# A kernel's order table of 1,771 steps replaced by another, with new durations in its planner

## The chip, the cores and the metric

The kernel runs on one core of a Trainium2 chip. The metric is the device time of one execution in microseconds (us). Besides its times there is one execution that the hardware profiler recorded; its page and its trace are quoted below.

## The reference

Two parts follow each other. The first is a linear attention with a decaying state (r, k, v, w: 4 batches, 8 heads, 768 tokens, 48 channels; u: one row for each head):

```python
for t in range(S):
    cur = np.einsum('bhd,bhe->bhde', u[None] * kt, vt)
    y[:, :, t] = np.einsum('bhd,bhde->bhe', rt, state + cur)
    state = wt[:, :, :, None] * state + np.einsum('bhd,bhe->bhde', kt, vt)
...
x = attn_out.transpose(0, 2, 1, 3).reshape(B * S, H * D)   # 3072 x 384
h = x @ w_in                                               # 384 x 2048
g = h * np.clip(h + 3.0, 0.0, 6.0) / 6.0
return g @ w_out                                           # 2048 x 384
```

Everything is float32; the weights arrive as 64-bit floats and are turned into float32 on the chip.

## The kernel before

**Work.** The tokens are cut into 24 chunks of 128 (`i`), four of which make a block (`bk`, six of them). For a chunk the kernel scans the decays backwards and forwards (`back`, L431; `fore`, L440), multiplies them onto k and r (`K`, L451; `R`, L455), works out the token's own term (`own`, `dot`, `sum`, `diag`: L464, L476, L482, L492), the scores inside the chunk (`score`, L501; masked into place by `above`, L508), turns K round (`turn`, L517; copied by `turned`, L522), multiplies it with v (`kv`, L601; copied by `kvs`, L612) and carries the state (`decay`, `mid`, `decb`, `state`: L530, L538, L546). The chunk is read out by L579 and L588. For chunks 0 and 1 this is `first`, after `clear` (L652) has started the accumulation and before `read` (L660) has put the last heads in place through a copy by ACT (`third`, L646).

**The two big products.** Block 0 computes them plainly (`up0`, L717, one step for each of 16 column groups and part of the tokens; `ramp` and `gate`, L707 and L728, are the activation; `down0`, L736). The five other blocks use fewer products on sums of the operands: 20 products for each half d of the columns (`up1.0.*`, `up1.1.*`, L832), whose results ACT and DVE add together (`read`, L847 and L849) before the activation (`clip`, `gate`, L853 and L857), and 7 products for the second weight (`down`, L887) on sums made by DVE (`sum`, L872). The sums of the weights themselves are made once by DVE (`sin`, L779 to L783; `sout`, L808). Each weight comes in 8 pieces: `fetch` (SP, L394) loads one into one of three `bits` buffers, ACT makes two halves of it (`low`, `sign`: L403, L408), DVE a third (`shift`, L414) and joins them (`full`, L418). Late in the program weights and decays are loaded again and looked at for values that the fast path cannot take (`vet`, L935).

**What sets the order.** Each piece of work is a step of a `Plan`: an engine, a planned duration, the steps that it needs, the buffers it holds. `Plan.order` does not search: it reads for each step its place from the table `ORDER` (two characters a step) and lays all steps in that sequence. Every engine then runs its own steps in it, one after another; a step that waits holds up all that stand behind it on its engine. SP's queue of loads is one of these engines. The planned durations, `RATE` (a load of kb kilobytes takes kb/RATE in the plan) and `LAND` give planned starts. With a given table these have one use only: before a PE step that is planned to start in the first 60 us, `Plan.emit` puts products of the identity with itself, whose result nobody reads (`spin`, L1269), one after another as long as the planned gap lasts. So the durations decide how many spins are in the program, and the table decides everything else.

There are four PSUM buffers called `bank`; an `up` holds one until its `gate` has read it, a `score` two until `above` has.

```python
rank = [CODE.index(ORDER[2 * i]) * 64 + CODE.index(ORDER[2 * i + 1]) for i in range(len(steps))]
...
out = [n for _, n in sorted(zip(rank, steps))]
...
while now < self.start[n] - 0.12:
    self.spin()
    now += next(us_ for upto, us_ in self.SPIN if now < upto)
```

Of the kernel before, what the change touches and what calls it, by code (L numbers as in the profile page):

```python
# [86 lines left out]
    "HVHiHWHyH2H9IrJWJlJtJ0GHHdGIG/HmItIyHGGtHNIPIVJcIDINIHIYIcKMLfLkG3IKG9HzILI/JCH3HZHjJeJjLnIvJbIwJgJiLxMAMLMWMQHnJdHo"
    "JvJ4K/LDJ1IBIdLqLuMIKTLtLwL1MRMfMmI4LlI6KHLmL6MBKOJUJnMFMPMpL4MJMbMiMwOrO5PAPHLHMGLKLrMHMZMeLyLZL0MtMxO1MYMrL9MvMzM5"
    "PFP5QELSMnLVMNMoM/NGMUL2MTOyPEP9M3O4M2PkPlPoQQQXQcQrQkNWO0NYOOOzPTPXOUN2OBP8QAQdPLQDPMQHQKQRQyRARHN+P/OAPdP+QWQaPhOc"
    "PNQlQpRLQVQoQYQqQtQuRtScSpSuS2ODQeOGQCQfQ8RCQMPQQGRQRTSkQ2RNQ4RXRZRdTZURUZRERIRMRgRmR9SCRlR0SDSiSxUWRwSnRxT/UBUDUjUx"  # L90
    "VCVIVMR3SjR5S0TKTyT2S8SSSdUeUhU3TgUVTeUbUdUiVKVUVdSIUYSLTUUXUwU0TYSmS6U2U+VfUpU7UuU/VDVJVyYEYGYUYKSVU4SbUfU5VPVSUlS/"
    "UmVkVpYHVOVbVRVmVqYOYRYYT6VcT7VAVeV3V9VHUoVEYMYQYcV2YLV6YNYSYfYiYkYrYnBCABAEArAuAsA2AGA4A7AwBAAHBDBHA6BPBBB1B+B7CFCD"
    "ClCoCmCwA0CTCZBrChBLCHCKCQC6CVC0C5DNDSD8EhEmEfEsDPDzD2D1EcCgD/EBDQEkCsDfDiDpDtEpE/FCE+FgEGErEvEwE2E1FKFOFLFVDvE3E6En"
    "FABGBMBWB3B8B/EUEbEiBZBhBtBkBxB0FaFhFiBbBiBoBnCCCPEAEIELBEBKBYBsByB2EHEPERB6CECIEeEoEuBwB5B9ExFIFRCMCeCjENESEWCfCtCz"
    "EQEVEYC3C/DEFSFYFbC8DIDOElEtEyCkCxDFD0D7ECCqDbDhEaEgEjDJDTDaG+HKHQDUDeDmE4E9FDDlDxD3EqEzE7DdDnDrD5EFEME8FBFHFjFtF0F6"
    "F/GCGEGBGFGKGMGRGbGeGmGuGvGsGwGyG4HBHJHUHaHrH6HgHlHqHwH1H5ICIGITIXD4D6FEFGFJFNFTFqGOGQGTGUHDHEHFHIHLHSHTHfHpHtHuHvHx"
    "H4H7H8H+IAIRIUIWIaIgIhIjIkIlInJNJPFsF1GAGGGJGLKDKhIFIOIpI5IeIuI2JGJqI+JAJLIQISI7IMIiImIZIzJDJOJRJkIqI0IxIbI8IsI9JEIo"
    "IfJYJQI3JBJIJVJXJpJ5KBKFJZKAJTJrJFJKJwJzJ6J9JMJSI1JHJ7KIKdKkKrJaJfKuJ+KEKXJmJxKGJuJ2KCKUKSKaJ/KRKKJsKiKJKYKqJ3JyKoKz"
    "J8KcKLKjKVKmKxK0K4KZKeK5K9KfKlKsKvKpKtKwK1KPKbKNLOLMLULCLGLLLYKnLAK2LELILNLQLTLWLaLbLjL3L5LFLJLXLRLcLpL8LdL+LeLhLvMC"
    "LgLiL/MMKgKyLoLsK7K8L7MDMKMOMXMaMlM8K3LzMSLBMVMgNBMdNDMkMsMyM9NPNTNcNmNvNpNrN1MqNANeMuM4NHM1NJNQNjNXNiNRNZNVM0NfNLNb"  # L100
    "NwNCM6NqN6NONlNUNuNdNyN3OQOqNhNkOKOTNoNsNtN0N4OLNzOFNaNgN9OHOSOhOpOXOaOjNxN5OPN7OCOMNENNOeOxOmO2OEONOIN/OZOROVOfOJNI"
    "OkOnOYOdOiO3OwO8PBPIPOPCPGOtO6OgOlOoOsO/PDOvO9OWObOuPjPJPqPVPZPgPtO7PRO+PYPePiPmPpPrPvPxP0P7QBPcPfPsPnP1P6QLP3QNPyP4"
    "QOQZPzP2QTQmPKPPQFQJPUPWQUQbQiQsQnQvQ1Q7PSQSQjPbQwQzQ+Q0Q/Q5RGRPRURSRcRkRvR7RFRKR4RoRrR1Q9RORYRVRhR/SRSUShRaRiRuRBRp"
    "RfRjRqRWRbR2R8RnR6SKSWSZSoSrStSySeSgSFSJSTSvSQSaS3S9RsSBRzSNSwS7TDTTTdSzS4TlSqSsTMR+SMSESGSYSlTFS+TJS1TBTASATISHTPTf"
    "SXSOTXTqSfTRS5TLTETNToTrTvTGTbTtTwTVTaTcTiTQTSTjTmTCTHTkTsT8UHT1T5UAUKTWT0TxT3T9UCUEUGUIULUMUUUgUqT4T+UJUFUNUcUtUPUv"
    "UOUSUkUrUQUTUzVGTOThUaUsTpTuUnU1U8VQVBVFVNVaTnUyU9TzVVVLViVYVlVXVhVoVtV1V8WZWiWsXNXQXbVgVjWEVnVxV4VrWBWPWVWWWdV5WCV/"
    "VsWeV+WFXVVzVwWmXhWIWOWTWgWYWhW0W4W8WaWcXlXnWQWSWpWuWkWoXYXcWDWGWlWvXEXLXTXmXpXzWMWRW2VuWHWJWXWfWnWyW9XHWrW1WwWAXIWN"
    "W6XrWKWbXOX3WjW7WtXKXBXMXXXaXfXDXFX4X6W+XCXRXUXPXSXsXuWzW3YPYXYeYmYVYZYhYqXqX7YWYdYAYFYjYlYoYuYsYtYxY8X+YgYpYJYyYvY/"
    "Y1ZBWqWxW/XoXZXgXkX1XAXWW5XeXvXwXiXxXtYIX2X5X9X/XdXjX0XyYTX8YBYaYbYCYDYwYzY3Y6ZDZHZLZOZoY2Y5ZcaPaWaeY0Y9ZMY7ZAZJZYZU"
    "ZfZGZKaZY4ZNZPZRZWZCY+ZTZgZEakZQZdZZZjZuZwZzZeZiZkZpanavZXZbZqZtZaZmabadZFZSZ+aKaYZ0Z7aCaTaaalZlZxZvZhZsZ8aGaEaNZIZV"  # L110
    "agZraDZyZ1Z9Z2ZnaOaFZ5araAaMaIaSacafaiaLaQaHaJawa0aRaUaVaXZ/aBajauZ3Z6aoa2amaqaya9Z4apahasa1a3axa6a4a+bFbKbNbPataza8"
# [1506 lines left out]
```

## Time and profile before

| | |
|---|---|
| time, median of 3 runs | 541.53 us (540.63 to 541.81) |
| the profiled execution's own time | 540.98 us |
| its span in the trace | 539.2 us |
| DVE busy | 416.1 us (77%) |
| ACT busy | 267.8 us (50%) |
| POOL busy | 116.1 us (22%) |
| loads and stores | 66.41 MB |

PE is TensorE, DVE VectorE, ACT ScalarE, POOL GpSimd; SP issues the loads. The span is shorter than the time by 1.8 us, which lie before the first and after the last recorded instruction. A float32 product stands in the trace as two records, so a spin is two. A record of a product runs on past the start of the next, so "busy" covers gaps of up to some 0.15 us; where PE's pace matters, it is read from the starts of consecutive groups.

### The profile page before, as it was taken

Reading aid. Unit: us, or ns where it says so; the run is one execution under the profiler, and the core shown is the slowest. Engines: PE = TensorE matmul, PEld = TensorE weight load, DVE = VectorE, ACT = ScalarE, POOL = GpSimd, SP = SyncE. Lnnn points to the kernel's source line nnn. Section 1 sums busy time; section 2 is a strip of 40 time slices with the busy share of each in tenths; the row PEclk is TensorE's granted clock in tenths of the full one; section 3 lists DMA queues with packets and bytes.
Section 4 is the critical chain, followed back from the end, with each engine's and each line's share of the span. In section 5 each row is a group of like instructions: output and inputs, shape, how many; then the busy total and the mean of one; then the engine's idle time right before and its main releaser. Section 6 shows DMA issues by size and latency. Waiting matters only on the chain.

```text
span 539.2 us, 13401 instructions
## 1 busy us (share of the span) xinstructions
PE 532.8 (99%) x5558; PEld 467.3 (87%) x5558; DVE 416.1 (77%) x709; ACT 267.8 (50%) x657; POOL 116.1 (22%) x111
## 2 busy tenths in 40 slices
PE   8999999999999999999999999999999999999997
...
GB/s 332 357 162 330 240 177 105 126 119 126 85 145 90 79 186 97 242 271 90 23 147 155 279 214 163 1 104 72 181 80 2 1 16 29 34 0 1 7 24 33
DMA packets 21458, 66.41 MB, mean 123 GB/s; under 512 B 3312, under 2 KB 11408, under 8 KB 21392
## 3 DMA queue, kind: packets, MB, share of 16 engines
...
q10 hardware_dynamic: 128, 0.00, 0.0%
...
## 4 chain that ended last, share of the span: by engine, by line
PE 93%; DVE 5%; issue 1%; ACT 0%; POOL 0%; POOLq 0%; DVEq 0%
PE bank L887 29%; PE bank L832 24%; PE bank L717 8%; PE bank L736 8%; PE bankS L887 5%; PE bankS L832 4%; PE y_ps L579 3%; PE ps L517 2%; PE bankS L1269 2%; PE y_ps L601 2%; PE bank L501 2%; PE y_ps L588 2%; DVE g L857 2%; DVE g L849 2%; PE ps L476 1%
## 5 line engine op out<-in xcount | busy, mean ns | idle before, releaser
L853 ACT ACTIVATE clip<-g,three 128x512 f32<-128x512 f32 x80 | 57.1, 721 | 54.8 <-DVE g L849 45.0
L849 DVE TENSOR_TENSOR g<-bank,g 128x512 f32<-128x512 f32 x80 | 53.7, 684 | 13.2 <-PE bank L832 10.3
L857 DVE SCALAR_TENSOR_TENSOR g<-clip,g 128x512 f32<-128x512 f32 x80 | 58.0, 739 | 7.5 <-ACT clip L853 7.5
L887 PE MATMUL bank<-w_out,g 128*128 128x192 f32 x320 | 57.3, 327 | 0.0
L492 ACT ACTIVATE A<-eyes,dg 128x64 f32<-128x64 f32 x192 | 49.5, 338 | 10.9 <-PE y_ps L588 10.6
L887 PEld LDWEIGHTS bank<-w_out,g 128*128 128x128 f32 x320 | 52.8, 190 | 1.2 <-DVE g L857 0.3
L451 POOL TENSOR_TENSOR K<-feat_in,E 112x512 f32<-112x512 f32 x17 | 22.0, 1294 | 138.1 <-PE bank L501 132.4
L684 ACT COPY xT<-y_ps 48x256 f32<-48x256 f32 x88 | 32.2, 365 | 27.7 <-PE y_ps L588 26.9
L717 PE MATMUL bank<-xT,w_in 128*128 128x256 f32 (+1 forms) x216 | 45.5, 362 | 0.0
L736 PE MATMUL bank<-w_out,g 128*128 128x384 f32 x128 | 43.8, 491 | 0.0
L832 PE MATMUL bank<-xT,w_in 128*128 128x256 f32 x160 | 40.4, 380 | 0.1
L717 PEld LDWEIGHTS bank<-xT,w_in 128*128 128x128 f32 x216 | 36.5, 190 | 4.5
L847 ACT COPY g<-bank 128x512 f32<-128x512 f32 x50 | 28.8, 581 | 20.8 <-PE bank L832 17.3
L736 PEld LDWEIGHTS bank<-w_out,g 128*128 128x128 f32 x128 | 23.5, 190 | 14.2
L905 ACT ACTIVATE o<-bank 128x192 f32<-128x192 f32 x30 | 9.9, 329 | 49.8 <-PE bank L887 49.6
L832 PEld LDWEIGHTS bank<-xT,w_in 128*128 128x128 f32 x160 | 30.0, 190 | 4.5 <-ACT g L847 0.7
L431 DVE TENSOR_TENSOR_SCAN E<-feat_in,back 112x520 f32<-112x520 f32 x24 | 31.4, 1308 | 3.0 <-POOL K L451 1.5
L455 POOL TENSOR_TENSOR W<-feat_in,W 112x512 f32<-112x512 f32 x17 | 24.0, 1411 | 43.0 <-DVE W L440 43.0
L440 DVE TENSOR_TENSOR_SCAN W<-feat_in,start 112x520 f32<-112x520 f32 x24 | 31.8, 1325 | 1.6 <-PE y_ps L579 1.4
L508 DVE COPY_PREDICATED A<-mask,bank 128x256 f32<-128x256 uint8 x48 | 18.6, 440 | 18.0 <-PE bank L501 18.0
L832 PE MATMUL bank<-xT,bits 128*128 128x256 f32 x120 | 30.9, 381 | 0.2 <-DVE A L508 0.2
L530 POOL TENSOR_TENSOR S<-S,w_min 112x192 f32<-112x192 f32 x15 | 11.3, 755 | 82.8 <-DVE S L538 82.8
...
## 6 DMA issues: line engine op xcount, KB each, us to landing
feat_in<-in_feat_dram SPq DMA_DIRECT2D x23, 772.5 KB, 4.4
bits<-in_moe_w_in_dram SPq DMA_DIRECT2D x8, 768.0 KB, 6.2
bits<-in_moe_w_out_dram SPq DMA_DIRECT2D x8, 768.0 KB, 5.2
feat_in<-in_moe_w_in_dram SPq DMA_DIRECT2D x8, 768.0 KB, 4.3
feat_in<-in_moe_w_out_dram SPq DMA_DIRECT2D x8, 768.0 KB, 5.1
...
v_in<-in_tok_dram SPq DMA_DIRECT2D x24, 192.0 KB, 4.3
feat_in<-in_wflat_dram SPq DMA_DIRECT2D x6, 768.0 KB, 4.5
```

The source lines that it names most:

```text
L431: nc.vector.tensor_tensor_scan(out=E_[:, ::-1], data0=d["w"][:, :0:-1], data1=back.rearrange("q p t -> q (p t)")[:, ::-1], initial=0.0, op ...
L440: nc.vector.tensor_tensor_scan(out=W_, data0=d["w"][:, :-1], data1=starts[i % 2].rearrange("q p t -> q (p t)"), initial=0.0, op0=ALU.mult, ...
L492: nc.scalar.activation(out=d["A"][:, h, :], in_=eyes, func=ACT.Copy, scale=d["dg"][:, h])
L684: nc.scalar.copy(out=blocks[bk]["xT"][g * GP:g * GP + D, :, at:at + HL], in_=st[i]["y_ps"][a][(g ^ a) * GP:(g ^ a) * GP + D, :, :])
L717: nc.tensor.matmul(h_ps[:, :(c1 - c0) * L], lhsT=w_in[:, f // 2, j, f % 2, :], rhs=b["xT"][:, j, c0 * L:c1 * L], start=(j == 0), stop=(j = ...
L736: nc.tensor.matmul(b["o", c][:, :DM], lhsT=g_of(0, f, c), rhs=w_out[:, f, :], start=(f == 0), stop=(f == NFC - 1))
L832: nc.tensor.matmul(b["p", d, c][:, z * HB:(z + 1) * HB], lhsT=weight(W_PLACE[r], d)[:, z, :], rhs=x_at(bk, X_PLACE[r]), start=fresh and z ...
L847: nc.scalar.copy(out=out_, in_=src)
L849: nc.vector.tensor_tensor(out=out_, in0=src, in1=out_of(bk, d, other), op=ALU.add if sign > 0 else ALU.subtract)
L853: nc.scalar.activation(out=c, in_=out_of(bk, d, u), func=ACT.Relu, bias=three, scale=twice)
L857: nc.vector.scalar_tensor_tensor(out=g, in0=blocks[bk]["r", d, u], scalar=6.0, in1=g, op0=ALU.min, op1=ALU.mult)
L887: nc.tensor.matmul(b["d", p, to][:, :h], lhsT=a, rhs=w(), start=(f == 0 and k in (1, 5)), stop=(f == HF - 1 and k in (2, 3, 4)), skip_grou ...
```

## The change

The table `ORDER` is replaced whole; it was found by a search that began at the old one. The planner's durations change with it: `RATE`, the scans, and the small state products.

```diff
 ORDER = (
-    "AAADAIAQAKAOALANAPARASAYAVAjATAXAZAdAmAqAfAoAzA3A/ACAFAWAiAcAnAbAaAeAgAhAlAtAyAkApAxA1A5A9A8A+BNBUBcAJAMBIBfBSBaBRBF"
...
+    "AAADAHAOAKAQAMANAPARASAkAWApATAYAcAhArAwAlAtA4A9BHACALAXAfAsAyAdAUAaAjAoAqA2A/AmAuAzBABEBjBGBJBTBYBkAFAIAgBFBpCGA7A+"
...
-    RATE = 270.0
+    RATE = 400.0
...
-            plan.add(f"back{i}", "DVE", 1.38, do(back_scan, i), ...
+            plan.add(f"back{i}", "DVE", 1.40, do(back_scan, i), ...
...
-            plan.add(f"fore{i}", "DVE", 1.155, do(fore_scan, i), ...
+            plan.add(f"fore{i}", "DVE", 1.18, do(fore_scan, i), ...
...
-                plan.add(f"decay{i}", "DVE" if dve else "POOL", 0.27 if dve else 0.5, do(decay, i),
+                plan.add(f"decay{i}", "DVE" if dve else "POOL", 0.27 if dve else 0.9, do(decay, i),
...
-                plan.add(f"mid{i}", "DVE", 0.27, do(middle, i), ...
+                plan.add(f"mid{i}", "DVE", 0.33, do(middle, i), ...
...
-            plan.add(f"decb{i}", "DVE" if dve else "POOL", 0.27 if dve else 0.5, do(decay_middle, i),
+            plan.add(f"decb{i}", "DVE" if dve else "POOL", 0.27 if dve else 0.9, do(decay_middle, i),
```

No step is added or taken away but spins: 38 before, 34 after. Of PE's 484 steps 329 stand at another place, of DVE's 614 532, of ACT's 437 358, of SP's 155 77, of POOL's 81 32; a PE step moves by 2.3 places on the mean, a DVE step by 4.8. Three places matter below.

The first is the start on the two engines that feed PE there. SP's loads (`feat_in`: r, k and w of a chunk; `v_in`: v of a chunk; `bits`: a piece of a weight), from the second chunk's on, before:

```order
L353 DMA feat_in<-in_feat_dram 128x1545
L365 DMA v_in<-in_tok_dram 128x384
L394 DMA bits<-in_moe_w_in_dram 128x768
L365 DMA v_in<-in_tok_dram 128x384
L394 DMA bits<-in_moe_w_in_dram 128x768 x2
L353 DMA feat_in<-in_feat_dram 128x1545
```

and after:

```order
L353 DMA feat_in<-in_feat_dram 128x1545
L365 DMA v_in<-in_tok_dram 128x384
L394 DMA bits<-in_moe_w_in_dram 128x768
L353 DMA feat_in<-in_feat_dram 128x1545
L394 DMA bits<-in_moe_w_in_dram 128x768
L365 DMA v_in<-in_tok_dram 128x384
L394 DMA bits<-in_moe_w_in_dram 128x768
L365 DMA v_in<-in_tok_dram 128x384
```

The third chunk's data stand three loads earlier, and v of the second chunk comes last of these. ACT's first rows, before (from `sum0` to the first weight piece):

```order
L482 COPY dg<-ps 128x8
L492 ACTIVATE A<-eyes,dg 128x64 x4
L522 COPY kn<-ps 128x448
L492 ACTIVATE A<-eyes,dg 128x64 x4
L458 COPY w_min<-E 112x8
L612 COPY kvs<-y_ps 112x384
L482 COPY dg<-ps 128x8
L492 ACTIVATE A<-eyes,dg 128x64 x8
L522 COPY kn<-ps 128x448
L403 ACTIVATE more<-bits 128x768
L408 ACTIVATE more<-bits 128x768
```

and after:

```order
L482 COPY dg<-ps 128x8
L492 ACTIVATE A<-eyes,dg 128x64 x4
L522 COPY kn<-ps 128x448
L403 ACTIVATE more<-bits 128x768
L458 COPY w_min<-E 112x8
L408 ACTIVATE more<-bits 128x768
L612 COPY kvs<-y_ps 112x384
L482 COPY dg<-ps 128x8
L492 ACTIVATE A<-eyes,dg 128x64 x12
L522 COPY kn<-ps 128x448
L403 ACTIVATE more<-bits 128x768
L408 ACTIVATE more<-bits 128x768
```

The first weight piece (L403, L408) has moved ahead of `kvs0` (L612), and a second piece now follows the second chunk's L522.

The second place is PE there, from the last spins ahead of `clear0` (L652) to `first0` (L579, L588), before:

```order
L1269 MATMUL bankS<-ident 128x128
L476 MATMUL ps<-u_col,rk 64x2 x8
L652 MATMUL y_ps<-xT,ident 128x256 x2
L1269 MATMUL bankS<-ident 128x128 x3
L517 MATMUL ps<-ident,K 128x112 x4
L1269 MATMUL bankS<-ident 128x128 x2
L579 MATMUL y_ps<-W,S 48x64 x8
L588 MATMUL y_ps<-A,v_in 48x64 x16
```

and after:

```order
L1269 MATMUL bankS<-ident 128x128 x4
L652 MATMUL y_ps<-xT,ident 128x256 x2
L517 MATMUL ps<-ident,K 128x112 x4
L1269 MATMUL bankS<-ident 128x128 x8
L579 MATMUL y_ps<-W,S 48x64 x8
L588 MATMUL y_ps<-A,v_in 48x64 x16
```

Five spins between `clear0` and `first0` have become eight. Further on, the six spins that stood ahead of the second L660 and one that stood near the ups are gone.

The third place is DVE in block 1, where it reads the products of the first half (L849: an addition that frees or shares a bank; L857 the activation's end, `gate`; L779 to L783 sums of weights; L935 and L484 a `vet` and a `sum` of a later chunk), before, up to the last read of that half but one:

```order
L849 TENSOR_TENSOR g_1972<-bank,g_1972 128x2x256
L857 SCALAR_TENSOR_TENSOR g_1972<-clip,g_1972 128x2x256
L849 TENSOR_TENSOR g_1972<-bank,g_1972 128x2x256
L849 TENSOR_TENSOR g_1984<-bankS,g_1984 128x2x256
L849 TENSOR_TENSOR g_1972<-bank,g_1972 128x2x256
L508 COPY_PREDICATED A<-mask,bank 128x4x64 x2
L538 TENSOR_TENSOR S<-S,kvs 112x192
L935 TENSOR_REDUCE w_max<-feat_in 128x1
L484 TENSOR_REDUCE dg<-rk 128x8
L849 TENSOR_TENSOR g_1984<-bankS,g_1972 128x2x256
```

and after, up to the last read of that half (L431 and L435 are a later chunk's `back`):

```order
L849 TENSOR_TENSOR g_1992<-bank,g_1992 128x2x256
L849 TENSOR_TENSOR g_1992<-bankS,g_1992 128x2x256
L779 SCALAR_TENSOR_TENSOR w_in<-w_in,S__1985 128x2x128
L857 SCALAR_TENSOR_TENSOR g_2000<-clip,g_2000 128x2x256
L783 TENSOR_TENSOR w_in<-w_in,S__1985 128x2x128
L431 SCALAR_TENSOR_TENSOR E<-feat_in,back 112x520
L435 RECIPROCAL start_79<-E 112x8
L779 SCALAR_TENSOR_TENSOR w_in<-w_in 128x2x128
L849 TENSOR_TENSOR g_1992<-bankS,g_2000 128x2x256
L779 SCALAR_TENSOR_TENSOR w_in<-S__1985,w_in 128x2x128
L508 COPY_PREDICATED A<-mask,bank 128x4x64 x2
L849 TENSOR_TENSOR g_2000<-bank,g_2000 128x2x256
```

From the first L849 of the half to its last, DVE had eleven reads, two sums of weights, five gates, the `vet`, a `sum` and a `mid` (L538) before; now it has eleven reads, nine sums of weights and one gate. Four gates, the `vet`, the `sum` and the `mid` come behind the last read. Seven more sums of weights stand inside.

More of the change, by code (lines that the diff above doesn't have):

```diff
@@ L87 @@
[L87 to L111, printed above, removed]
@@ new lines @@
+    "FsEaFuGEGJEhENFdFhGcGeG5F6GXF7GdGoG1HOHVHYHfHpD9GaF3GZGyG2F8FiGWGhG4G9HbGxHDG0HHHJHNHwH5IEFjG6FkGkG7HjHqGqGfGpHhHkIC"
+    "HSHoHgHzH3INIXJQJeJtJmGMHZGOHQHaInIsHUGtHCH+IAJgH2IRH6IVIZJyLjLnG8H/G/HtIII8JBHyHTHrJYJZLoIbJnIdJpJvL6L+MEMSMKHuJXHv"
+    "JWJfLILNJcIBIJLtLvMHJ3LxL1MLMTMbMhIyLqI2JlLpMCMMJrJJKDMJMQMlL9MOMUMyM5OxPBPMPHLGMFLHLsMGMaMkL4LTLyMmMrO3MYM0McM3M6NR"
+    "PKPzQFLbMiLdMRMoNBNIMXL7MVO6O9P8M9O2M+PhPmPpQTQcQiQpQuNbO5NeNwO4PUPXN0NyODP7QAQlPQP4PRQBQGQLQ1Q7RDNmP6NoPfP5QYQePjOH"
+    "PCQoQrRFQXQtQaQyQ0Q3RuSfSrSzS6NsQjN9QCQkQ6REQKPFQHRKRRSoQ5RBQ8RTRXRcTeURUdP9RCP/QnRISISPQxQOQvSpS8UWR1SlR3SsS9TYUqUy"
@@ L114 @@
+    "apZuZxZ2Z5aBZ8ZIZ9aLZ/a4aJaSaOaWaYaaafaRaTaNaPa5a7aAaDaZabaEaHarawZ3Z7aGazaialavbBaQakZ+anatayaxa9a3bCbDbIbObRaoaubA"
+    "a1bEbMbTa2bGbNbUbFbJbWbbbHbKbZbea6a8bSbVa/bLbXbabcbhbfbgbkbna+bYbdbPblbibpbQbmbjbqJIJwLQLYJ1KHKOLBMpM7MZMnMvNHNLNiNN"
+    "NpNCNXPqP3PbPnQgQzRNRkQ2RHRJReSBSURoR9VmV3VcVyU8VMVRViV+WHWNbo"
 )
@@ L1012, in fast_path @@
                          hold=[("rk_in", [f"own{i}"])])
-            plan.add(f"back{i}", "DVE", 1.38, do(back_scan, i), [f"feat{i}"] + [f"fore{i - 2}"] * (i > 1) + [f"back{i - 1}"] * (i > 0), k,
+            plan.add(f"back{i}", "DVE", 1.40, do(back_scan, i), [f"feat{i}"] + [f"fore{i - 2}"] * (i > 1) + [f"back{i - 1}"] * (i > 0), k,
                      [("E", [f"K{i}", f"least{i}"])], port=True)
@@ L1016, in fast_path @@
                      k + 0.1, [("K", [scored(i), turned_by(i)])], port=True)
-            plan.add(f"fore{i}", "DVE", 1.155, do(fore_scan, i), [f"back{i}"] + [f"fore{i - 1}"] * (i > 0), k + 0.2,
+            plan.add(f"fore{i}", "DVE", 1.18, do(fore_scan, i), [f"back{i}"] + [f"fore{i - 1}"] * (i > 0), k + 0.2,
                      [("W", [scored(i), read_by(i) if i < BC else f"begin{i}"])], port=True)
```

29 lines of the change are left out of this document (23 added, 6 removed).

## The prediction

> **What bounds the kernel now.** The page first: PE is busy for all of the span but 6.4 us, and in its slices only the first and the last fall short.
>
> ```profile
> span 539.2 us, 13401 instructions
> ...
> PE 532.8 (99%) x5558; PEld 467.3 (87%) x5558; DVE 416.1 (77%) x709; ACT 267.8 (50%) x657; POOL 116.1 (22%) x111
> ...
> PE   8999999999999999999999999999999999999997
> ```
>
> So a new order can win only three things: spins, which the page counts as work; waits of PE; and what is hidden in the overlap of records. The groups by line give the spins, the busy time by stages says who stands behind PE:
>
> ```profile
> L1269 PE MATMUL bankS<-ident 128*128 128x128 f32 x76 | 12.5, 318 | 1.4 <-POOL ident masks.py:199 1.4
> ```
>
> ```profile
> 0.00:20.00 20.00, 18.48 (x300) 16.98 (x302) 15.59 (x31) 12.46 (x34) 3.01 (x15) 1.00 0.92 347
> 20.00:40.00 20.00, 19.91 (x329) 18.08 (x329) 18.64 (x38) 18.71 (x52) 0.00 (x0) 1.00 0.61 217
> ...
> 160.00:180.00 20.00, 19.71 (x125) 16.54 (x125) 19.85 (x30) 11.52 (x22) 1.71 (x1) 1.00 0.25 83
> ```
>
> (Columns: stretch, length, busy PE, PEld, DVE, ACT, POOL with counts, granted clock, DMA share, GB/s.) The 38 spins cover 12.5 us, the largest loss of the kernel. From 20 us on DVE and ACT are within 7% of full: whoever puts a wait there shifts PE. At 160 us DVE is full. These are the two places where the order can matter: the start, and DVE in block 1. Elsewhere PE runs at its own pace, and the same products in another order cost the same.
>
> **The change, part by part. 1: the start.** The new table has four spins fewer. Those of the last long run took 1.44 us for six, start to start (23.37 to 24.81), 0.24 each, so by the count alone the start gains 1.0 us. That holds only if the data are there when the plan says. What the trace says of them:
>
> ```profile
> 1.43 5.97 PE L1269 MATMUL bankS<-ident 128*128 128x128 f32 x34 [1.43 <-POOL ident masks.py:199]
> ...
> 8.69 1.24 DVE L431 TENSOR_TENSOR_SCAN E<-feat_in,back 112x520 f32<-112x520 f32 x1 [0.18 <-DMA feat_in<-in_feat_dram]
> ...
> 9.28 0.53 ACT L522 COPY kn<-ps 128x448 f32<-128x448 f32 x1
> ...
> 11.19 0.48 ACT L612 COPY kvs<-y_ps 112x384 f32<-112x384 f32 x1 [0.32 <-PE y_ps L601]
> ...
> 12.03 1.13 PE L652 MATMUL y_ps<-xT,ident 112*128 112x256 f32 x4
> ...
> 12.35 2.02 ACT L492 ACTIVATE A<-eyes,dg 128x64 f32<-128x64 f32 x8
> ...
> 13.00 0.83 PE L1269 MATMUL bankS<-ident 128*128 128x128 f32 x6
> ...
> 13.67 0.55 PE L517 MATMUL ps<-ident,K 112*128 112x112 f32 x4
> ...
> 14.05 0.62 PE L1269 MATMUL bankS<-ident 128*128 128x128 f32 x4
> ...
> 14.61 0.65 PE L579 MATMUL y_ps<-W,S 48*48 48x64 f32 x16
> ...
> 14.69 1.07 ACT L403 ACTIVATE more<-bits 128x768 uint16<-128x768 uint32 x1
> ...
> 15.62 1.07 ACT L408 ACTIVATE more<-bits 128x768 bf16<-128x768 int32 x1
> ...
> 16.54 0.51 ACT L646 COPY xT<-y_ps 48x128 f32<-48x128 f32 x2
> ...
> 17.64 1.45 PE L660 MATMUL y_ps<-xT,S__114 112*128 112x64 f32 x12
> ```
>
> ```profile
> 23.37 1.60 PE L1269 MATMUL bankS<-ident 128*128 128x128 f32 x12
> 24.81 1.45 PE L660 MATMUL bank<-xT,S__114 112*128 112x64 f32 x12
> ```
>
> ```profile
> 9.00:17.00 8.00, 7.91 (x220) 6.97 (x219) 6.57 (x14) 7.16 (x23) 0.00 (x0) 1.00 1.03 418
> ```
>
> ```profile
> feat_in<-in_feat_dram SPq DMA_DIRECT2D x23, 772.5 KB, 4.4
> bits<-in_moe_w_in_dram SPq DMA_DIRECT2D x8, 768.0 KB, 6.2
> ...
> v_in<-in_tok_dram SPq DMA_DIRECT2D x24, 192.0 KB, 4.3
> ```
>
> The second chunk's data land at 8.6 (DVE's scan starts at 8.69 after a wait for them). Behind them the queue moves 418 GB/s: a weight piece (768 KB, 0.786 MB) takes 1.88 us, a chunk 1.89, its v 0.47. The new plan gives a piece 546/400 = 1.37 us: half a microsecond too little each time. By the rows: first piece 8.6 + 0.47 + 1.88 = 10.95.
>
> Now ACT. Before, its first piece is turned at 14.69, long after it landed, and `kvs0` (L612) runs at 11.19. After, the piece stands ahead of `kvs0`: ACT is free at 9.8, waits until 11.0, spends 2.0 us on L403 and L408 (14.69 to 16.54 and the `w_min` copy between), and `kvs0` ends at 13.5, not 11.67. `clear0` (L652) needs it, and PE's queue stands behind `clear0`: 13.55 for 12.03. Then come `clear0` (0.97, 12.03 to 13.00), `turn1` (0.38) and eight spins, which run whether they are needed or not: 8 x 0.24 = 1.9. `first0` starts at 16.8 for 14.61.
>
> `read0` (L660) waits for `third0` (L646). ACT gets there after `kvs0` at 13.5, twelve L492 (0.25 each by the row of eight: 3.0), L522 (0.5), and a second weight piece. That piece's load has two chunks' data and a piece before it: 10.95 + 1.89 + 1.88 + 0.47 + 1.88 = 17.1; L403 and L408 end at 19.0, L646 at 19.5. `read0` at 19.55 for 17.64: **1.9 us late**. The Trainium skill, "DMA: Bandwidth & Descriptors", section "Where 436 GB/s comes from", says that the HBM side, some 358 GB/s for a core, binds loads like these; the trace disagrees, with 418. By 358 the six loads to that piece would take 9.9 us for 8.5 and `read0` would be 1.4 us later still.
>
> From `read0` to the second L660 PE took 7.17 us before (17.64 to 24.81), 1.44 of it spins. After, there are none, and the `turn` of chunk 2 (0.4) stands there: 7.17 - 1.44 + 0.4 = 6.1, so 25.7. It is 0.9 later with 0.4 of work ahead: **0.5 us behind**.
>
> Next, up to 57 us. Before, PE's ups run there without a gap:
>
> ```profile
> 29.98 4.11 PE L717 MATMUL bank<-xT,w_in 128*128 128x128 f32 x24
> ```
>
> After, `shift3` stands on DVE behind the second gate and ahead of two scans. Its piece is the seventh load after 17.1 (v, chunk, piece, v, chunk, piece, piece): 2 x 0.47 + 2 x 1.89 + 3 x 1.88 = 10.4, so 27.4. DVE would be there at 26.5 and waits 0.9. Behind it are both scans (1.24 each) and the gate that frees the fifth up's bank, so PE, which has four banks, meets that wait in full or, with a margin, not at all: 0 to 0.9. I take 0.7, since DVE and ACT have 7% idle at most.
>
> Start: +0.5 + 0.7 = **+1.2 us**. Ends: -1.0 (the plan is right and only spins go) and +1.9 + 0.9 = +2.8 (nothing after `read0` is won back).
>
> **2: DVE in block 1.** PE in the second half's first products, and the chain that ended last, in the same stretch:
>
> ```profile
> 155.18 1.13 PE L832 MATMUL bank<-xT,apart 128*128 128x256 f32 x4 [0.51 <-DVE g L849]
> ...
> 163.17 1.13 PE L832 MATMUL bank<-T__1912,w_in 128*128 128x256 f32 x4
> ```
>
> ```profile
> 153.92 0.60 DVE g L857
> ...
> 156.89 0.35 DVE S L538
> 157.25 1.47 DVE w_max L935
> ...
> 158.83 0.54 DVE dg L484
> 159.37 0.60 DVE g L849
> ```
>
> ```profile
> 235.65 10.44 PE bank L832 x48
> ```
>
> ```profile
> L783 DVE TENSOR_TENSOR w_in<-w_in x2: 416/420/425, 115.5 to 139.2; 128x256 f32<-128x256 f32 x2
> ```
>
> Between the two PE rows stand 32 products. At the pace of an undisturbed run (10.44/48 = 0.2175) that is 6.96 us; it took 7.99. With the 0.51 ahead of it PE loses 1.5 us here, waiting for reads (L849) that stand on DVE behind gates (L857) and a `vet` (L935). After, four gates (2.4), the `vet` (1.47), a `sum` and a `mid` (0.9) come behind the half's last read, seven sums of weights (0.42 each by the last row, 2.9) come in: the last read is some 1.9 us earlier after the first. What comes out lies before the second half's reads, where DVE has 0.15 us free in 20; part of the wait can come back there. I take **-1.2**, ends -1.5 and 0.
>
> **3: the rest.** Two more waits have such a cause:
>
> ```profile
> 328.93 1.13 PE L832 MATMUL bank<-xT,bits 128*128 128x256 f32 x4 [0.23 <-DVE A L508]
> ```
>
> ```profile
> 374.53 1.57 PE L887 MATMUL bank<-top,S__4083 128*128 128x192 f32 x8 [0.19 <-DVE S__4083 L872]
> ```
>
> They are 0.4 us together; each may go or come elsewhere: 0, ends -0.5 and +0.5. POOL's 32 moved steps cost nothing: it is idle for 78% of the span, and PE waits for it only at 1.43. The durations alone cost nothing beyond their spins.
>
> **Sum:** 540.98 + 1.2 - 1.2 = 541.0 for an execution like the profiled one. That one lies 0.55 below the median of the runs shown; on the median's scale, 541.53 + 0.0 = **541.5 us**.
>
> **The rivals.** *A, the plan comes true:* waits at the start are absorbed, four spins go (-1.0), block 1 is mended (-1.5), and one of the small waits (-0.2): 541.53 - 2.7 = 538.8. For it: the old start has spins that PE did not need (it spins at 13.00 though `kvs0` is done at 11.67). Against it: the landing at 10.95. *B, waits for weight pieces rule the start:* ACT and DVE, in order, stand behind loads that land 1.2 us or more after the engine is ready; nothing is won back, +2.8, and block 1 gives 0.5: 541.53 + 2.3 = 543.8. It decides as soon as `kvs0` ends after 13 us and a DVE wait for a piece follows near 27. *C, the clock:* the first 34 products took 5.97 us, 0.176 each, later ones 0.12 (12 in 1.44). Should a wait at the start make PE slow again for as many products, it costs 34 x 0.056 = 1.9 us: 543.4. My longest wait of PE is 1.6 us (the four spins ahead of `clear0` end near 11.9), and the trace holds none as long after the first spin. The Trainium skill, "TensorE: Matmul & The Clock Gate", section "Part 1: The HAM clock gate", has the clock fall to half after an idle window of some 3.4 us; by it 1.6 us would do nothing, and no row here shows such a fall.
>
> **How the numbers follow.** Forecast (within 1.1 us of 541.5) 0.38; A 0.33; B 0.25; C 0.04. The range reaches past A's half and B's: 539.0 to 543.7. A measurement of this kernel tells about 0.2% (1.1 us) from no change; faster by more is A, 0.33, slower is B and C, 0.29, the same 0.38.
>
> **What would show it.** After, the row of L612 near 13 us and L652 behind it near 13.5; L660 near 19.5 and 25.7; a DVE wait for `bits` near 27; in block 1 no gap of PE ahead of the first L832 of the second half. I am wrong if L612 runs near 11 us (the load is faster than 418 GB/s), if PE idles for over a microsecond between 27 and 60 us, or if DVE's waits in later blocks take over from those of block 1.

## The result and the profile after

| | before | after |
|---|---|---|
| median of 6 runs | 541.33 us (540.63 to 541.81) | 551.0 us (549.48 to 552.29) |
| ratio, 95% interval | | 1.0177 [1.0157, 1.0197] |
| the profiled execution's own time | 540.98 us | 551.47 us |

The change costs 9.7 us. It was forecast as no change (541.5, at most 543.7). The page of after: span, busy times of the engines, PE in 40 slices of 13.7 us, and the shares of the chain of work that ended last.

```profile
span 549.7 us, 13382 instructions
...
PE 533.5 (97%) x5550; PEld 465.7 (85%) x5550; DVE 413.5 (75%) x709; ACT 267.7 (49%) x657; POOL 111.4 (20%) x111
...
PE   7999989999999999999999999999999999999997
...
PE 70%; DMA 14%; DVE 10%; ACT 3%; issue 2%; SPq 1%; POOL 0%; DVEq 0%; ACTq 0%
```

PE is about as long busy as before (533.5 for 532.8) and now idle for 16.2 us instead of 6.4: nearly all of the loss is waiting. The slice in which it falls short, besides the first and the last, is the sixth (69 to 82 us). 14% of the chain are loads. The same line of the page of before names none:

```profile
PE 93%; DVE 5%; issue 1%; ACT 0%; POOL 0%; POOLq 0%; DVEq 0%
```

The waits of PE in after (engine and line that waits <- the one waited for: us in total, times, the longest):

```profile
PE bank L717 <- DVE g L728: 2.4, 2, 1.7
PE bank L832 <- DVE A L508: 2.3, 2, 2.0
...
PE bank L832 <- DVE g L849: 1.3, 2, 0.9
PE bank L736 <- DVE g L728: 1.1, 1, 1.1
```

Before, PE's waits for DVE came to 0.9 us in all. What PE waits for is mostly DVE; and those of DVE's own waits that end with a load are, in the same view of after:

```profile
DVE top L414 <- DMA bits<-in_moe_w_out_dram: 5.8, 3, 2.3
...
DVE words L942 <- DMA feat_in<-in_moe_w_in_dram: 3.1, 3, 1.5
...
DVE words L942 <- DMA feat_in<-in_moe_w_out_dram: 2.6, 4, 1.6
```

L414 is `shift`, the third of a weight piece; L942 is `vet`, which looks at a weight loaded again. Before, these rows were 0.2 us and none. How they reach PE is read from the chain of after between 55 and 92 us, in order of time (start, us of the chain, what):

```profile
48.95 7.76 DMA bits<-in_moe_w_out_dram
...
56.73 0.56 DVE top L414
57.29 2.28 DVE W L440 x2
...
63.62 0.48 DVE top L414
64.10 0.02 SPq L394
...
64.15 6.29 DMA bits<-in_moe_w_out_dram
...
70.54 0.56 DVE top L414
...
73.48 0.29 DVE g L728
...
76.89 0.15 ACT clip L707
77.04 6.49 DMA bits<-in_moe_w_out_dram
...
85.45 3.03 PE bank L736 x8
```

This is a circle. A `shift` waits for its piece (56.73, after a wait of 1.69). The next one (63.62) waits for nothing, but it comes late behind the first; when it has run, its `bits` buffer is free, and only then can SP issue the next piece (64.10). That one lands 6.29 us later; two chunks, issued at 60.51 and 62.31, are in the queue ahead of it. DVE's next `shift` stands there (70.54, after a wait of 2.31) with scans, sums and the gate at 73.48 behind it, for which PE waits 1.71. The plan gives such a load 546/400 + 1.9 = 3.27 us behind its issue, if nothing is ahead of it in the queue. The third turn goes through ACT, the other reader of a `bits` buffer, which DVE's lateness holds up too: the load is issued at 77.04 and lands at 83.53, and PE's wait of 1.14 ends at 85.45.

Where the 9.7 us arise is told by a lag: how much later PE has done the same amount of product work as in before. It is worked out from all rows of PE in two traces (each group's own pace from start to start, spins counted as nothing), so no row shows it; it is good to a few tenths. In us, at the time in the column's head, for the runs that are told of below:

| profiled run | 20 | 50 | 60 | 100 | 150 | 180 | 260 | 420 | 520 |
|---|---|---|---|---|---|---|---|---|---|
| after | 2.3 | 1.6 | 2.4 | 6.6 | 6.7 | 7.4 | 9.2 | 10.8 | 10.7 |
| new_then_old_from_begin6 | 2.0 | 0.6 | 2.2 | 5.6 | 5.6 | 5.5 | 5.6 | 5.6 | 5.6 |
| old_then_new_from_begin6 | -0.6 | -0.6 | -0.6 | -0.5 | -0.4 | 1.8 | 2.6 | 3.5 | 3.4 |
| new_small_reloads | 2.3 | 1.5 | 2.4 | 6.7 | 6.7 | 9.0 | 9.4 | 9.6 | 9.4 |
| old_start_then_new | -0.7 | 0.2 | 4.1 | 6.4 | 6.5 | 7.2 | 8.2 | 10.1 | 10.0 |
| new_shifts_moved | 2.3 | 0.7 | 0.7 | 0.5 | 0.5 | 1.3 | 1.9 | 2.5 | 2.5 |
| old_vet_twice | 0.0 | 0.0 | 0.0 | 0.0 | 0.0 | 1.5 | 1.5 | 1.3 | 1.3 |
| joined_three | -1.1 | -2.1 | -1.9 | -1.5 | -1.7 | -2.9 | -1.1 | -1.1 | -1.1 |

After loses 2.3 us at the start (of which 1.6 are left at 50), about 5 between 50 and 100, 0.7 in block 1, 1.8 to 260 and 1.6 to 420.

**Theory ("loads"):** the new table was searched with loads that land too early, so steps stand ahead of their landing, and engines that work in order hold everything behind them. **Rivals:** the numbers and the spins themselves; DVE asked for the wrong work first, with no load involved; late losses that only follow from the early ones.

### The profile page after: what moved, and what is told of

Its sections match the earlier page's. It is cut to its first block, busy times and chain, and to the rows that moved or that the text cites. A ratio compares the mean times of both kernels' runs of the same rounds, so it can differ in the third digit from the quotient of the medians.

```text
span 549.7 us, 13382 instructions
## 1 busy us (share of the span) xinstructions
PE 533.5 (97%) x5550; PEld 465.7 (85%) x5550; DVE 413.5 (75%) x709; ACT 267.7 (49%) x657; POOL 111.4 (20%) x111
## 4 chain that ended last, share of the span: by engine, by line
PE 70%; DMA 14%; DVE 10%; ACT 3%; issue 2%; SPq 1%; POOL 0%; DVEq 0%; ACTq 0%
PE bank L887 27%; PE bank L832 19%; PE bank L736 8%; PE bankS L887 5%; DMA feat_in<-in_moe_w_out_dram 4%; DMA bits<-in_moe_w_out_dram 4%; DMA bits<-in_moe_w_in_dram 3%; PE bankS L832 3%; DMA feat_in<-in_moe_w_in_dram 2%; PE y_ps L579 2%; PE y_ps L601 1%; PE y_ps L588 1%; PE bank L501 1%; DVE words L942 1%; DVE g L849 1%
## 5 line engine op out<-in xcount | busy, mean ns | idle before, releaser
L857 DVE SCALAR_TENSOR_TENSOR g<-clip,g 128x512 f32<-128x512 f32 x80 | 55.1, 702 | 9.2 <-ACT clip L853 8.9
L849 DVE TENSOR_TENSOR g<-bank,g 128x512 f32<-128x512 f32 x80 | 53.3, 684 | 8.6 <-PE bank L832 5.9
L455 POOL TENSOR_TENSOR W<-feat_in,W 112x512 f32<-112x512 f32 x17 | 25.6, 1505 | 55.1 <-DVE W L440 55.1
L440 DVE TENSOR_TENSOR_SCAN W<-feat_in,start 112x520 f32<-112x520 f32 x24 | 29.9, 1253 | 6.6 <-PE y_ps L579 6.6
L905 ACT ACTIVATE o<-bank 128x192 f32<-128x192 f32 x30 | 9.8, 327 | 51.2 <-PE bank L887 51.2
L431 DVE TENSOR_TENSOR_SCAN E<-feat_in,back 112x520 f32<-112x520 f32 x24 | 30.8, 1282 | 3.7 <-DMA feat_in<-in_feat_dram 2.1
L530 POOL TENSOR_TENSOR S<-S,w_min 112x192 f32<-112x192 f32 x15 | 13.5, 902 | 85.6 <-DVE S L538 85.6
L508 DVE COPY_PREDICATED A<-mask,bank 128x256 f32<-128x256 uint8 x48 | 18.5, 440 | 13.9 <-PE bank L501 10.7
```

Of the source, the lines that this page charges most:

```text
L431: nc.vector.tensor_tensor_scan(out=E_[:, ::-1], data0=d["w"][:, :0:-1], data1=back.rearrange("q p t -> q (p t)")[:, ::-1], initial=0.0, op ...
L440: nc.vector.tensor_tensor_scan(out=W_, data0=d["w"][:, :-1], data1=starts[i % 2].rearrange("q p t -> q (p t)"), initial=0.0, op0=ALU.mult, ...
L849: nc.vector.tensor_tensor(out=out_, in0=src, in1=out_of(bk, d, other), op=ALU.add if sign > 0 else ALU.subtract)
L857: nc.vector.scalar_tensor_tensor(out=g, in0=blocks[bk]["r", d, u], scalar=6.0, in1=g, op0=ALU.min, op1=ALU.mult)
```

## The experiments

"Old" and "new" are the two tables. All kernels below have the new durations, except old_vet_twice.

**Old table, new durations; and the two tables cut in two.**

```diff
 ORDER = (
-    the new table
+    old_table_new_durations: the old table
+    old_then_new_from_begin6: its first 418 steps, the others in the new order
+    new_then_old_from_begin6: 430 steps of the new table, the others in the old order
```

> The old table with the new durations: nothing differs from the kernel before but the spins (34 for 38). Theory 'loads' (the new table puts work of ACT and DVE ahead of the landing of what it needs): 541.3, within 1.0. Rival 'spins and durations' (fewer spins or the planner's numbers carry the loss): 545 to 551. Rival 'order of DVE itself' (no load is involved, DVE is simply asked for the wrong thing first): 541.3 as well.

> The first 418 steps of the old table (to the read-out of the seventh chunk, some 95 us), all others in the order of the new one. The lag of the profiled run after the change, read at equal work of PE, grows by 2.3 us to 20 us, by 4.3 between 60 and 90, by 1.0 at 165, 1.5 at 250 and 1.2 at 410. Loads, and also order of DVE itself: only what lies behind 95 us is left, 3.7: 545.0, between 544 and 546. If the loss of the later places follows from the lateness of the first 90 us and not from their own order: 541.5.

> The mirror image: the new table up to the read-out of the seventh chunk (430 steps), the rest in the order of the old one. Both theories on the order: the loss of the first 90 us alone, 541.3 + 6.6 = 547.9, between 547 and 549. If the later losses are consequences of the first: 551.

Measured: 540.22 us (ratio 0.9991 [0.9981, 1.0]), 544.66 (1.0074 [1.0058, 1.0091]) and 547.20 (1.0128 [1.0105, 1.015]), beside 540.97 of before. The durations and the four spins do no harm; that rival falls. The two halves cost 3.7 and 6.2 us, and 9.9 is about the whole: the later part of the new table loses time behind an old start too, so the late losses are not all consequences of the early one. That the halves add up so well is in part luck. All four runs of old_then_new_from_begin6 show a clock of 0.996 or 0.997, and in the profiled one the clock is 0.87, 0.50 and 0.78 in the three windows of 2 us from 158 us on: 0.85 x 2 = 1.7 us of its lag of 3.4. From 180 to 420 us it loses 1.7 by the table, where after loses 3.4. What makes up the other half is not shown.

**Small re-loads.**

```diff
-                nc.sync.dma_start(out=t, in_=src)
+                nc.sync.dma_start(out=t[:, :m // 12], in_=src[:, :m // 12])
...
-            hi = t.bitcast(I32).rearrange("p (j two) -> p j two", two=2)[:, :, 1]
+            n_ = t.shape[1] // 12
+            hi = t[:, :n_].bitcast(I32).rearrange("p (o j two) -> p o j two", o=1, two=2)[:, :, :, 1].to_broadcast([128, 12, n_])
```

> The new table; of each weight that is loaded again late in the program only a twelfth of the columns comes, and the check on DVE reads these twelve times over, so its count and length of instructions stay and only the 786 KB of each of these 16 loads shrink to 66 KB. The kernel then looks at a twelfth of the weights only. Loads: the waits of DVE for these loads near 240 and 400 us go, 551.0 - 2.7 = 548.3, and DVE's waits for feat_in at its L942 vanish. Order of DVE itself: 551.0, within 0.7.

Measured: 548.61 us (1.0138 [1.0121, 1.0154]), 2.4 less than after, for 2.7 expected. L942 no longer stands among DVE's waits for a load. Against the trace of after, PE gains 1.4 us between 240 and 260 and 1.4 between 400 and 420, at the two places where `vet` had waited. In between the profiled run has a loss that was not expected: 2.3 us in block 1. Three windows of it (stretch, length, busy PE, PEld, DVE, ACT, POOL with counts, granted clock, DMA share, GB/s):

```profile
166.00:168.00 2.00, 1.89 (x6) 1.66 (x7) 2.00 (x3) 1.14 (x3) 0.00 (x0) 0.71 0.04 12
168.00:170.00 2.00, 2.00 (x6) 1.56 (x6) 1.97 (x5) 0.93 (x2) 0.89 (x1) 0.50 0.10 25
170.00:172.00 2.00, 2.00 (x39) 1.44 (x37) 2.00 (x3) 0.47 (x1) 0.00 (x0) 0.93 0.29 47
```

and the first two of them in after:

```profile
166.00:168.00 2.00, 1.90 (x9) 1.73 (x10) 2.00 (x3) 1.12 (x3) 0.00 (x0) 1.00 0.05 12
168.00:170.00 2.00, 2.00 (x28) 1.51 (x30) 1.97 (x5) 1.03 (x3) 0.89 (x1) 1.00 0.10 25
```

In both runs PE has waited 1.96 us just before, ahead of 166.1. In one the clock stays at 1.00, in the other it falls to half. Three of the six runs of after show a mean clock of 0.997 too, untraced; in the profiled run of old_then_new_from_begin6 the fall told of above stands behind the same wait (1.95 us, for L508).

**Only the start undone; only one step of the start undone.**

```diff
 ORDER = (
-    the new table
+    old_start_then_new: the first 144 steps of the old table, the others in the new order
+    new_kvs0_first: the new table with low0 and sign0 (L403, L408) behind kvs0 (L612) on ACT
```

The planned starts move with the steps, and the spins with them: old_start_then_new has 38, new_kvs0_first 41, for the 34 of after.

> The first 144 steps of the old table (to some 45 us), all others in the order of the new one. If the start's loss (2.3 us to 20 us, of which 1.6 to 2.4 are left at 50 us) adds to that of 60 to 90 us: 551.0 - 2.0 = 549.0. If the loads between 45 and 90 us set their own times, whatever PE had gained before: 551.0, with longer waits of DVE for bits between 55 and 85.

> The new table with kvs0 ahead of the first weight piece on ACT, as before the change (L612 ahead of L403 and L408), nothing else. L612 then ends near 11.7 for 13.6 and L652 starts near 12. If that one step makes the start's loss: 551.0 - 1.9 = 549.1. If the second piece ahead of L646 holds read0 anyway (L660 at 19.84), the two are worth 0 to 0.5: 550.5 to 551.

Measured: 550.15 us (1.0156 [1.0135, 1.0177]) and 551.67 (1.0202 [1.0173, 1.0231]). The 2.3 us of the start are worth under 1 us: the lag of old_start_then_new is 0.2 at 50 us and 4.1 at 60. Its timeline there, of ACT and of PE (start, us, engine, line, operation, [idle before <- releaser]):

```profile
51.73 1.08 ACT L403 ACTIVATE more<-bits 128x768 uint16<-128x768 uint32 x1 [1.95 <-DMA bits<-in_moe_w_out_dram]
...
54.78 0.60 PE L517 MATMUL ps<-ident,K 112*128 112x112 f32 x4 [1.83 <-ACT dg L482]
```

ACT stands before a weight piece for 1.95 us with the copies behind it, one of which PE needs; the wait that stood at the start of the program has moved to the next load. Behind this wait, too, the clock fell in the profiled run, so about 1.8 of these 4.1 us are the clock's (0.40 and 0.50 of 2 us each); its windows:

```profile
56.00:58.00 2.00, 2.00 (x6) 1.40 (x6) 2.00 (x3) 2.00 (x4) 0.00 (x0) 0.60 0.14 33
58.00:60.00 2.00, 2.00 (x19) 1.56 (x19) 2.00 (x6) 1.87 (x7) 0.00 (x0) 0.50 0.03 8
60.00:62.00 2.00, 2.00 (x6) 1.21 (x4) 1.04 (x3) 1.64 (x7) 0.00 (x0) 0.50 0.83 241
```

The three other runs, at clock 1.00, lie between 548.9 and 550.93. In new_kvs0_first L612 runs early, and `read0` is no earlier:

```profile
11.33 0.48 ACT L612 COPY kvs<-y_ps 112x384 f32<-112x384 f32 x1 [0.52 <-PE y_ps L601]
...
17.22 1.07 ACT L403 ACTIVATE more<-bits 128x768 uint16<-128x768 uint32 x1 [0.23 <-DMA bits<-in_moe_w_in_dram]
...
19.13 1.16 PE L1269 MATMUL bankS<-ident 128*128 128x128 f32 x8
20.12 1.45 PE L660 MATMUL y_ps<-xT,S__114 112*128 112x64 f32 x12
```

The second piece, at 17.22, holds `third0` (L646) until 19.60 and with it L660; four spins hold L660 for another 0.4 us. Most of what PE won at L652 (11.96 for 13.65) went into spins as well: 13 stand between L652 and L579, where after has eight, and L579 comes at 16.29 for 16.87.

**The shifts.** Sixteen steps of DVE, `shift0` to `shift15`, stand elsewhere in the new table: counted against DVE's other steps, seven stand 1 to 8 places later, four 1 to 9 earlier, five where they were (the counts in the expectation are too high). The places were sought for loads as the traces show them. Those that were moved up free their buffer sooner.

```diff
 DVE, fore4 to gate0.11.0
-shift12  fore4  fore5  gate0.14.0  R4  gate0.13.0  mid4  gate0.11.0
+fore4  fore5  gate0.14.0  R4  shift12  gate0.13.0  mid4  gate0.11.0
```

> The new table, in which only the 16 steps 'shift' of DVE (L414, the ones that wait for a piece of a weight) stand elsewhere: by 0 to 17 places on DVE, most of them later than the landing that the trace shows, three earlier where their piece has long landed. Loads: most of the 4.3 us lost between 60 and 90, and a part of the start: 551.0 - 4.5 = 546.5, between 545 and 548; DVE's waits for bits at L414 fall from 11 us to under 5. Order of DVE itself (too much work of DVE in this stretch, whatever it waits for): 550 to 551.

Measured: 547.0 us median of seven (1.0096 [1.007, 1.0123]), but 542.79 and 543.24 in the two runs at clock 1.00. In the profiled one of these the loss between 50 and 100 us is gone whole: its lag is 0.5 at 100 us for 6.6. From 180 to 420 us it loses 1.2 for 3.4, so the shifts undo a part of the late losses as well. DVE's waits for loads in it:

```profile
DVE words L942 <- DMA feat_in<-in_moe_w_out_dram: 1.3, 3, 0.7
...
DVE top L414 <- DMA bits<-in_moe_w_in_dram: 0.4, 1, 0.4
```

The row for the second weight (5.8 us) is not there any more. With the amount of DVE's work unchanged, the rival "too much DVE work" is out for this stretch. The other five runs (546.25 to 548.12) show clocks of 0.991 to 0.997.

**Block 1, with the shifts and without.**

```diff
 DVE, from the 13th chunk's back scan
+above10  (L508)
 back12  (L431, L435)
 sin1.19  (L779)
 read1.0.a18  (L849)
 sin1.20  (L779)
-above10  (L508)
```

> The new table with one step of DVE moved up by five places: 'above10' (L508, at 165.5 us in the profiled run) stands ahead of the scan, two sums of weights and a read that stood before it. Order of DVE itself: PE's wait of 1.96 us ahead of 166.10 shrinks by 1.0 to 1.9, and with it goes the clock of under 1.00 that half the runs show: 549.0, between 548.3 and 550. Loads: no load is waited for there, 551.0. Rival: the reads behind it become late by as much as it became earlier (0.8), and PE waits for them: 550.5 to 551.

> The new table with the 16 shifts moved as before and, besides, above10 five places earlier on DVE. In new_shifts_moved two of seven runs held clock 1.00 (542.8, 543.2), five fell to 0.991 to 0.997 (546.3 to 548.1), and PE waited 1.9 us at 160. If that wait lets the clock fall: without it all runs hold 1.00 and lie near 543, at most 544. If the spread has another cause: runs up to 548 again, median 546 to 547.

Measured: 550.36 us (1.015 [1.0119, 1.018]) and 543.74 (1.0055 [1.0034, 1.0077]). In the first, L508 runs at 162.35 and the wait of 1.96 is gone, but PE then waits

```profile
166.94 1.13 PE L832 MATMUL bank<-xT,w_in 128*128 128x256 f32 x4 [1.13 <-ACT g L847]
...
170.38 1.13 PE L832 MATMUL bankS<-T__1895,w_in 128*128 128x256 f32 x4 [0.32 <-ACT bankS L840]
```

and the lag at 180 us is 7.4 as in after. The rival holds: what is late next is as late. Still the step is worth something: in shifts_and_above10 five of six runs lie between 543.11 and 543.97 at 0.999 or 1.00, and one at 546.59 (0.997), where new_shifts_moved had five of seven at 546 to 548. The wait of 1.9 us cut into pieces costs PE the same. With it cut, two of ten runs of these two kernels show a clock of 0.997 or below, without (after and new_shifts_moved) eight of thirteen: this points to fewer falls and does not settle it.

**A wait alone.** The kernel before, with 1.74 us of DVE added in block 1:

```diff
-                nc.vector.tensor_reduce(out=w_max[:, j:j + 1], in_=t, axis=AX.X, op=ALU.max, apply_absolute_value=True)
+                for _ in range(2 if j == 0 else 1):
+                    nc.vector.tensor_reduce(out=w_max[:, j:j + 1], in_=t, axis=AX.X, op=ALU.max, apply_absolute_value=True)
```

> The kernel before with the first vet of DVE (L935, 1.74 us at 157.16) done twice. DVE is full there, so PE waits up to 1.7 us longer between 158 and 165, in one piece or in three: 543.0. If a wait of 1.5 us or more lets the clock fall: some runs below 1.00 and at 544 to 545. If the waits come in pieces under 1 us and only long ones count: all runs at 1.00, 542 to 543. If DVE makes it up: 541.4.

Measured: 544.63 us (1.0062 [1.0048, 1.0077]). One run at clock 1.00: 542.28. Three at 0.997: 544.29, 544.98, 545.01. Its timeline, DVE and PE:

```profile
157.12 3.53 DVE L936 TENSOR_REDUCE w_max<-feat_in 128x1 f32<-128x1536 f32 x2
...
162.44 1.13 PE L832 MATMUL bank<-T__1912,bits 128*128 128x256 f32 x4 [1.86 <-ACT bankS L840]
```

The wait of 1.86 us costs 1.0 in the one run in which the clock holds (before: 541.24), and 2.0 to 2.7 more in the others; no run of before lies below a clock of 0.998. None of the three was traced: that the fall stands behind this wait is inferred from the other kernels' traces.

**new_shifts_moved once more.**

> The kernel new_shifts_moved once more, for its trace. By its seven runs it falls below clock 1.00 in about five of seven. If it does: a stretch of some 3 us at half clock behind the wait of 1.9 us near 160, and the rest of the 3 to 5 us in waits that follow from it, or in a second such stretch. If not: near 543.

One run: 543.14 us at 0.999. It shows no run of the other kind, so where the 3 to 5 us of those five runs lie is open; a mean clock of 0.997 by itself is 0.003 x 540 = 1.6.

**Is there anything to be won?** First, the start of the old table's kind with the shifts moved (`kvs0` ahead of the first piece, `third0` ahead of the second, on ACT):

> The same with two more moves on ACT in the start: kvs0 ahead of the first weight piece, third0 (L646) ahead of the second. If these two pieces make the start's 2.3 us: L660 near 18.0 for 19.8, and 1 to 1.5 us less than shifts_and_above10. If the pieces behind them, then later, are missed as much: no less.

545.80 us (1.0082 [1.0057, 1.0108]): a miss. L660 came at 19.07, only 0.8 earlier than in after, and its second run at 26.50, 0.4 later. The kernel has 42 spins: 13 stand between L652 (11.90) and L579 (16.23), two just ahead of the second L660, so a part of what ACT gave PE was spun away. Other waits came in (1.11 us at 467.9). Then tables searched with loads as measured:

> A table searched from the old one, all steps free, with loads as the traces show them: 418 GB/s and 1.8 us to 42 us, 320 GB/s from there, each order judged a second time with 270 GB/s, 2.0 us and all work of DVE and ACT 3% longer. 23 spins for 34. If loads were what the plan of the change had wrong: faster than both kernels, 537 to 540 (up to 1.5 us at the start, 1.5 in block 1, the small waits). If there is more in it (order of DVE, the clock): 541 or above.

> The same search, begun at the new table with the shifts moved; 34 spins. The same two readings: 537 to 540, or 541 or above.

547.04 us (1.0131 [1.0084, 1.0178]) and 542.93 (1.0036 [1.0011, 1.0061]): misses both. The first is 1.7 us ahead of before at 50 us and behind from 240 on, by PE's waits for reads, for sums and for a `vet`. The second is 1.9 ahead at 180 and even at 520, and its span is still 2.0 longer; three copies of results (L905) stand behind PE's last product, for one before. The parts that were ahead were then joined:

```diff
 ORDER = (
+    joined_three: searched_from_old to 90 us, searched_from_new to 187 us, then the old order
+    joined_two: searched_from_new to 187 us, then the old order
+    joined_seam_246, joined_seam_228: joined_three with its second seam at 246 and 228 us
```

> The order of searched_from_old to the first product of block 0's second chunk (down0.1.0, some 90 us), then that of searched_from_new to 187 us, then the old table. From the lags of those two runs: -1.4 at 90 us, a further -1.3 to 187, nothing behind it: 541.4 - 2.7 = 538.7, between 538 and 540. If parts don't add up because each order holds what the one before it made late: 541 to 543.

> The order of searched_from_new to 187 us, then the old table. From its lag of -1.9 at 180 and the tail of the kernel before: 541.4 - 1.7 = 539.7, between 539 and 541. If the parts don't add up: 541 to 543.

> joined_three with its seam to the old table at some 246 us for 187. The wait of 0.9 at the seam goes, that of 0.4 stays: 2.9 - 0.8 = 2.1 ahead of before: 539.2, between 538.3 and 540. If the seam loses as much wherever it is: 540.3.

> The same with the seam at some 228 us: 539.2, between 538.3 and 540; if the seam loses as much wherever it is: 540.3.

| | median | ratio, 95% interval | runs at clock 0.995 or below |
|---|---|---|---|
| joined_three | 540.34 | 0.9993 [0.9971, 1.0014] | 2 of 12 |
| joined_two | 541.71 | 1.0007 [0.9998, 1.0016] | 0 of 11 |
| joined_seam_246 | 542.11 | 1.0029 [1.0008, 1.0051] | 7 of 12 |
| joined_seam_228 | 541.20 | 1.0015 [0.9996, 1.0035] | 4 of 11 |

None is faster than before. At clock 1.00 joined_three has ten runs between 539.31 and 540.75, whose median is 1.2 below that of before; but its 2.9 us of lead at 180 fall to 1.1 at the seam, where PE waits

```profile
197.84 2.87 PE L887 MATMUL bank<-bits,S__2368 128*128 128x192 f32 x16 [0.88 <-DVE A L508]
```

and moving the seam brought runs of up to 546 and 550 us at clocks down to 0.984. The three with low clocks share a start with 23 spins; joined_two, with 34, never fell below 0.999. Whether fewer spins let the clock fall is open: the two starts differ in their order too, new_shifts_moved fell in five of seven runs with 34 spins, and no trace of a run with a low clock was taken here.

## Why the prediction was wrong

**The forecast, no change, is wrong, and the step that failed is the third:** "Elsewhere PE runs at its own pace, and the same products in another order cost the same", with 0 and ends of 0.5. It held before, because the old table had its waits for loads off DVE's way (L414 0.2 us, L942 none). It was then taken over for a table of which 532 of 614 DVE steps had moved. The loads were walked through in the stretch to 57 us, up to the piece forecast for 27.4, and no further, and L414, DVE's step on a weight piece, was looked at there alone. The view of before by stages had a sign of more, in rows that the prediction did not print:

```profile
40.00:60.00 20.00, 19.75 (x295) 16.16 (x294) 19.41 (x39) 18.95 (x46) 0.00 (x0) 1.00 0.83 312
60.00:80.00 20.00, 20.00 (x117) 16.24 (x116) 19.36 (x41) 16.95 (x31) 0.00 (x0) 1.00 0.60 201
```

DVE is 97% busy from 40 to 80 us, fuller than in the row of 20 to 40 us for which the prediction said that a wait there shifts PE. Between 50 and 100 us the waits of `shift` for pieces cost 5.0 us (new_shifts_moved: gone), those of `vet` for the weights loaded again, near 250 and 410 us, 2.4 (new_small_reloads). That the new `RATE` was off was seen ("half a microsecond too little each time"), with 418 GB/s of a queue that always has the next load. Behind 57 us it often hasn't: a load is issued when a buffer comes free. The page's median times from issue to landing in after are:

```profile
bits<-in_moe_w_out_dram SPq DMA_DIRECT2D x8, 768.0 KB, 6.4
feat_in<-in_moe_w_in_dram SPq DMA_DIRECT2D x8, 768.0 KB, 4.7
```

The plan has 3.27 for the first and 800/400 + 1.9 = 3.9 for the second from the end of the issue when nothing is ahead in the queue, so 3.72 and 4.35 with its 0.45 for the issue. With 270 GB/s these are 4.37 and 5.31. The medians hold the time behind other loads too, so not all of the 6.4 is the rate's. The two pieces issued at 70.29 and 76.07, when the load before had landed or all but landed, took 4.3 us each. For such pieces the old `RATE`, wrong as a rate of the full queue, is the nearer one; for `feat_in`, at 4.7, the new one is no worse. The Trainium skill, "SBUF — State Buffer", section "The DMA setup-cost knee", gives a transfer some 2 us and its bytes at 436 GB/s; an estimate from that page is 3.8 us for 0.786 MB, 0.5 below the 4.3 of these two pieces.

**The start (+1.2)** was walked rightly and weighed wrongly. In after:

```profile
13.05 0.45 ACT L612 COPY kvs<-y_ps 112x384 f32<-112x384 f32 x1
...
13.65 1.10 PE L652 MATMUL y_ps<-xT,ident 112*128 112x256 f32 x4 [1.12 <-ACT dg L482]
...
19.84 1.52 PE L660 MATMUL y_ps<-xT,S__114 112*128 112x64 f32 x12
...
26.11 1.46 PE L660 MATMUL bank<-xT,S__114 112*128 112x64 f32 x12
...
33.38 1.74 PE L717 MATMUL bank<-xT,w_in 128*128 128x128 f32 x12 [0.69 <-DVE g L728]
```

Forecast were 13.5 for the end of L612 (13.50), 13.55, 19.55 and 25.7 for the three PE rows, and 0.7 for the wait; DVE's wait for `bits`, forecast near 27 with 0.9 us, is 1.62 us ahead of 28.69. The lag at 50 us is 1.6 for 1.2. But undoing the start wins only 0.9: behind it the loads decide, and what PE gains it waits for again at 54.78.

**Block 1 (-1.2)** failed by its sign: +0.7 at clock 1.00. The rows of after, PE and DVE:

```profile
163.11 1.03 PE L832 MATMUL bank<-T__1895,w_in 128*128 128x256 f32 x4
166.10 1.10 PE L832 MATMUL bank<-xT,apart 128*128 128x256 f32 x4 [1.96 <-DVE A L508]
...
162.42 1.23 DVE L431 TENSOR_TENSOR_SCAN E<-feat_in,back 112x520 f32<-112x520 f32 x1
...
164.69 0.90 DVE L779 SCALAR_TENSOR_TENSOR w_in<-S__1985,w_in 128x256 f32<-128x256 f32 x1
165.52 0.76 DVE L508 COPY_PREDICATED A<-mask,bank 128x256 f32<-128x256 uint8 x2
```

The gates and the `vet` went behind the reads, as the step said, and the reads are early. But PE here needs two banks that L508 has to empty, and L508 had come to stand behind a scan and the sums of weights. The step counted how much DVE work lay ahead of the reads, and not which DVE step PE meets next.

**The rivals.** B had the mechanism, ACT and DVE in order behind pieces that have not landed, in the wrong place (up to 27 us) and at a third of its size. C came near the price of a fall of the clock (1.9 us; 2.0 to 2.7 measured), though by another reckoning, 34 slow products; the longest wait that it foresaw was 1.6 us, at the start, and it was waits of 1.8 to 2.0 us further on behind which the clock fell. The Trainium skill, "TensorE: Matmul & The Clock Gate", section "Part 1: The HAM clock gate", has the clock fall after an idle window of some 3.4 us that runs freely; that the same wait counts in one run and not in the next agrees with a free-running window, that 1.9 us are enough does not agree with a whole idle one. A, the plan come true, did not happen, and of the tables made here with better load times none is faster than the kernel before.
